# Issuing the output stores of a channel-attention and gated-convolution kernel from ScalarE's queue instead of SyncE's

## The chip, the core and the metric

The kernel runs on one core of one Trainium2 chip. The time is device microseconds for one execution of the program; the figure for a kernel is the median of its runs. In the profile, PE is TensorE, PEld its weight loads, DVE VectorE, ACT ScalarE, POOL GpSimd and SP SyncE; "SPq" and "ACTq" are instructions that SP and ACT carry out in their own queues, above all the issuing of transfers, and they aren't counted as busy time.

## The reference

Two stages, one behind the other, for 4 batches of 6336 rows and 256 channels, in float32:

```
qn = q / (norm(q, axis=1) + 1e-06);  kn = k / (norm(k, axis=1) + 1e-06)
s = kn.transpose(0, 2, 1) @ qn / tau            # 256 x 256 per batch
a = softmax of s over its last axis
x = v @ a                                       # 6336 x 256 per batch
gate = sigmoid(sum over 5 taps of conv_w[k] * x shifted by 4 - k rows)
out = (gate * (x @ w_val)) @ w_out
```

## The kernel before

The first stage takes q and k in groups of three blocks of 128 rows. For each group, ACT rounds the data to the format that TensorE multiplies fast (`hi`, L435), POOL computes the remainder (`lo`, L438), PE adds the products hi·hi, hi·lo and lo·hi to `s_ps` (L494), ACT squares the group (L462), and DVE or POOL adds the squares (L466). At the end of a batch a chain of small operations on ACT, DVE, POOL and PE turns `s_ps` into the softmax and into the two matrices that the second stage multiplies by: L544 and L546 on PE, a square root on ACT (L562), reciprocals on DVE, the exponential (L588) and the division (L600) on ACT, a transposition on PE (L613), and so on. Square root, exponential and sigmoid each need an own function table on ACT, so going from one to another costs an ACT_TABLE_LOAD.

The second stage runs in 52 steps of at most 508 rows, 13 for each batch. The steps of batch b run interleaved with the first stage of batch b+1. A step loads v in four transfers (L690), DVE transposes it (L695), ACT rounds it (`v_hi`, L699), POOL takes the remainder (`v_lo`, L702), PE makes `x_ps` and `val_ps` (L710), ACT starts the convolution (L733) and DVE (with some help from ACT and POOL, L741 and L744) adds the taps (L736), ACT takes the sigmoid (L747), DVE multiplies by `val_ps` (L754), ACT rounds (`g_hi`, L760), POOL takes the remainder (`g_lo`, L763), and PE makes the output in two halves (`o_ps`, L782). ACT copies each half from PSUM to the tile `o_sb` (L791), and when both halves are there, two transfers store the step: one of 112 partitions and one of 15 (L796). The step before the last is stored half by half. The last step, of 240 rows, has its own copies and stores (L801, L803), one half on ACT and one on DVE and SP.

No line of the program orders this by hand. Each piece is a task with an engine, an estimated cost, its dependencies and the tile buffers that it takes and uses. A planner (`Plan.run`) gives each task a due time, worked out backwards from the order in which PE should do its work, and then places tasks engine by engine: of those that can start, the one due first. The order found in this way is the order of the instructions in each engine's queue, and each queue runs strictly in order. A task that issues transfers has its cost as a tuple (bytes, transfers, slowness); the planner counts 0.45 us of the issuing engine for each transfer. The number of `o_sb` buffers is 2, of q/k buffers (`raw`) 7, of `v_raw` 4, of `hi`/`lo` and of `v_hi`/`v_lo` 3 each.

```
task(("Y", n, p), "ACT", 0.48, lambda p=p: out_copy(p), deps=[("F", n, p)] ...)
task(("R", n), "SP", (w * C * 4, 2, 1), lambda: store(0, nt), deps=[("Y", n, p) ...], uses=[o_i])
```

One thing about transfers is needed below. Each transfer signals its end on one of eight semaphores, which show as DMAHW0 to DMAHW7 in the listing of waits; they are dealt out in turn over all transfers of the program, whichever queue issues them. A transfer that gets a semaphore waits until the transfer that had it before, eight places earlier in the program, has landed; the waiting is done by the queue that issues it.

Of the kernel before, what the change touches and what calls it, by code (L numbers as in the profile page):

```python
# [27 lines left out]
class Plan:  # L28
# [6 lines left out]
    def task(self, key, engine, cost, emit, deps=(), uses=(), takes=(), lead=(), table=None):  # L35
        assert key not in self.tasks, key
        self.tasks[key] = dict(key=key, engine=engine, cost=cost, emit=emit, deps=list(deps), lead=dict(lead), table=table, uses=list(dict.fromkeys(list(uses) + list(takes))),
                               takes=list(takes), order=len(self.tasks))
# [182 lines left out]
def kernel(  # L221
# [13 lines left out]
    nc = tc.nc  # L235
    B, N, C = q.shape
# [34 lines left out]
    task = plan.task  # L271
# [396 lines left out]
    def even(rows):  # L668

        whole_ = rows // 16 * 16 if rows % 15 else rows  # L670
        return [x for x in ((0, whole_), (whole_, rows)) if x[0] < x[1]]

    def step_tasks(n):

        b, i = all_steps[n]
        t0, w = chunks[i]
# [3 lines left out]
        t = {}  # L680
# [84 lines left out]
        nt = -(-w // P)  # L765
        rows = w // nt
        pairs = [range(j, min(j + (1 if end else 2), nt)) for j in range(0, nt, 1 if end else 2)]
# [17 lines left out]
        dst = out[b, t0:t0 + w].rearrange("(j r) c -> r j c", j=nt)  # L785
# [7 lines left out]

        def store(a, z):
            for r0, r1 in even(rows):
                nc.sync.dma_start(out=dst[r0:r1, a:z, :], in_=t["o_sb"][r0:r1, a:z, :])  # L796

        def out_end(u):
            copy, dma = ((nc.scalar.copy, nc.scalar), (nc.vector.tensor_copy, nc.sync))[u]
# [5 lines left out]
        v_i, vs_i, gate_i, g_i, o_i = ("v_raw", n), ("v", n), ("gate", n), ("g", n), ("o_sb", n)  # L805
# [4 lines left out]
        for h in range(NH):  # L810
            x_i = (("s_ps", "acc_ps")[h] if late else "x", n, h)
            if edge:
                task(("E", n, h), "DVE", 0.08, lambda h=h: margin(h), deps=[("M", b, "divide")] + ([("X", n - 1, h)] if n else []), uses=[x_i], takes=[x_i])
            task(("X", n, h), "PE", 1.385 * part, lambda h=h: mix(h), deps=[("W", n), ("M", b, "low")] + ([("E", n, h)] if edge else []),
                 uses=[vs_i, x_i], takes=[] if edge else [x_i],
                 lead={("W", n): first_lo if new else last_lo, ("M", b, "low"): last_lo if new else 0} if h == 0 else {})
            task(("G", n, h), "ACT", 0.06 + 0.51 * part, lambda h=h: gate(h), deps=[("X", n, h), ("ready", "conv")] + [("G", n, x) for x in range(h)],
                 uses=[x_i, gate_i], takes=[gate_i] if h == 0 else [])
# [5 lines left out]
            for k_ in range(1, few):  # L824
                task(("D", n, h, k_), "DVE", 0.08 + 0.57 * part, lambda h=h, k_=k_: tap(h, k_),
                     deps=[("D+", n) if few < K else ("G", n, h) if k_ == 1 else ("D", n, h, k_ - 1)] + ([("D", n, h, k_ - 1)] if few < K and k_ > 1 else []),
                     uses=[x_i, gate_i])
# [6 lines left out]
        if n >= NS - 2:  # L834
            for h in range(NH):
# [3 lines left out]
                     deps=[("H", n, h)], uses=[gate_i, g_i])  # L839
# [5 lines left out]
        for p in range(len(pairs)):  # L845
# [3 lines left out]
                 uses=[g_i, o_ps_i], takes=[o_ps_i], lead={x: (0.47 * len(pairs[p]) if HEADS else 0.47) for x in low_done} if p == 0 else {})  # L849
# [3 lines left out]
                task(("Y", n, p), "ACT", 0.48, lambda p=p: out_copy(p), deps=[("F", n, p)] + [("Y", n, x) for x in range(p)], uses=[o_ps_i, o_i], takes=[o_i] if p == 0 else [])  # L853
        if n == NS - 2:
            for p, pair in enumerate(pairs):
                task(("R", n, p), "SP", (len(pair) * rows * C * 4, 2, 1), lambda pair=pair: store(pair[0], pair[-1] + 1), deps=[("Y", n, p)], uses=[o_i])
        elif not end:
            task(("R", n), "SP", (w * C * 4, 2, 1), lambda: store(0, nt), deps=[("Y", n, p) for p in range(len(pairs))], uses=[o_i])
        t["pairs"] = [("F", n, p) for p in range(len(pairs))]
        return t["pairs"]  # L860

# [6 lines left out]
    for b in range(B):  # L868
        softmax_tasks(b)
    outs = [step_tasks(n) for n in range(NS)]  # L870


# [85 lines left out]
```

## Time and profile before

| | |
|---|---|
| time, three runs | 591.70, 591.97 and 593.29 us, median 591.97 |
| the profiled execution | 593.26 us, its span from first to last instruction 591.5 us |
| DVE busy | 514.3 us, 87% |
| TensorE's granted clock | 1.000 over the span |
| transfers | 105.83 MB; the 16 DMA engines are at 8 to 9 tenths in the first quarter of the span and at 2 to 6 tenths in the last |
| the chain that ended last | 89% PE, 6% DMA, 1% each of ACT, POOL, issuing and SP's queue |

The chain of work that ended last goes through loads of q, k and v until 58.6 us; from there to the end of PE's work it is PE and nothing else.

### The profile page before, as it was taken

The page shows a single profiled execution, that of the slowest core. Times are in us where ns is not written, and L with a number is a line of the kernel's source. Part 1 is how long each engine was busy: PE and PEld are TensorE (multiplying, and loading weights), DVE is VectorE, ACT ScalarE, POOL GpSimd, SP SyncE. Part 2 cuts the span into 40 slices and gives each one's busy share as a digit, 9 for nine tenths or more (in the row PEclk, how much of TensorE's full clock was granted, in tenths as well). Part 3 has the DMA queues.
Part 4 walks back from the last instruction along what each step waited for, and adds up shares of the span by engine and source line. Part 5 has one row for each costly group of instructions (what it writes and reads, how often), then busy time and mean ns, then how long its engine had stood idle before and what let it go on. Part 6 is the DMA issues. An engine that isn't in the chain of part 4 may idle for free.

```text
span 591.5 us, 10511 instructions
## 1 busy us (share of the span) xinstructions
PE 585.7 (99%) x3667; PEld 531.2 (90%) x3667; DVE 514.3 (87%) x792; ACT 479.6 (81%) x582; POOL 506.3 (86%) x241
## 2 busy tenths in 40 slices
PE   9999999999999999999999999999999999999997
PEld 8898899998989999998989998998998998888887
DVE  3996899999989899988788899988969989988774
ACT  6698989889899979787798989788559777767754
POOL 4997999999997999999887999999935778777743
PEclk9999999999999999999999999999999999999999
DMA  8999997958577797874766899678333464553214
GB/s 331 383 368 231 273 243 200 213 133 226 169 157 179 203 214 195 169 190 112 219 166 153 208 213 244 143 190 181 75 93 103 114 160 118 124 141 89 68 40 123
DMA packets 154943, 105.83 MB, mean 179 GB/s; under 512 B 111114, under 2 KB 137994, under 8 KB 154890
## 3 DMA queue, kind: packets, MB, share of 16 engines
q1 hardware_dynamic: 154467, 104.51, 68.7%
q8 instruction: 29, 0.48, 0.4%
q10 hardware_dynamic: 423, 0.65, 0.3%
q14 instruction: 24, 0.20, 0.1%
HBM read 79.18 MB, written 25.95 MB: 178 GB/s over the span
## 4 chain that ended last, share of the span: by engine, by line
PE 89%; DMA 6%; ACT 1%; POOL 1%; issue 1%; SPq 1%; DVE 0%; POOLq 0%; ACTq 0%
PE o_ps L782 24%; PE x_ps L710 23%; PE val_ps L710 23%; PE s_ps L494 17%; DMA raw<-in_q_dram 4%; PE o_ps L626 1%; DMA raw<-in_k_dram 1%; DMA v_raw<-in_v_dram 1%; ACT sq L462 1%; SPq L412 1%; PE o_ps L613 0%; POOL v_lo L702 0%; ACT hi L435 0%; POOL acc L466 0%; PE o_ps L546 0%
## 5 line engine op out<-in xcount | busy, mean ns | idle before, releaser
L736 DVE SCALAR_TENSOR_TENSOR gate<-x_ps,wa,gate 128x508 f32<-128x508 f32 (+1 forms) x400 | 271.2, 717 | 33.9 <-ACT gate L733 31.2
L438 POOL TENSOR_TENSOR lo<-raw,hi 128x1536 fp32r<-128x1536 f32 (+2 forms) x65 | 185.4, 2857 | 7.8 <-ACT hi L435 6.0
L702 POOL TENSOR_TENSOR v_lo<-v_raw,v_hi 128x1024 fp32r<-128x1024 f32 (+1 forms) x52 | 124.1, 2387 | 14.6 <-ACT v_hi L699 12.1
L763 POOL TENSOR_TENSOR g_lo<-gate,g_hi 128x1016 fp32r<-128x1016 f32 (+2 forms) x52 | 120.7, 2322 | 16.9 <-ACT g_hi L760 16.6
L466 DVE TENSOR_TENSOR acc_ps<-acc_ps,sq 128x512 f32<-128x512 f32 (+1 forms) x146 | 101.2, 693 | 21.0 <-ACT sq L462 17.1
L710 PE MATMUL x_ps<-v_hi,w 128*128 128x512 f32 (+2 forms) x416 | 110.1, 384 | 0.0
L710 PE MATMUL val_ps<-v_hi,w 128*128 128x508 f32 (+1 forms) x416 | 107.8, 380 | 0.0
L462 ACT ACTIVATE sq<-raw 128x1536 f32<-128x1536 f32 (+2 forms) x68 | 95.8, 1413 | 3.0 <-POOL acc L466 1.7
L435 ACT CAST hi<-raw 128x1536 fp32r<-128x1536 f32 (+2 forms) x65 | 78.9, 1216 | 19.8 <-PE s_ps L494 11.1
L710 PEld LDWEIGHTS val_ps<-v_hi,w 128*128 128x128 f32 x416 | 76.1, 188 | 14.9
L710 PEld LDWEIGHTS x_ps<-v_hi,w 128*128 128x128 f32 x416 | 72.9, 188 | 12.8 <-POOL w L607 0.4
L733 ACT ACTIVATE gate<-x_ps,wa 128x508 f32<-128x508 f32 (+1 forms) x104 | 68.5, 664 | 14.0 <-PE x_ps L710 13.7
L782 PE MATMUL o_ps<-wo_hi,g_hi 128*127 128x256 f32 (+1 forms) x396 | 79.3, 282 | 0.0
L782 PE MATMUL o_ps<-wo_lo,g_hi 128*127 128x256 f32 (+1 forms) x396 | 79.0, 281 | 0.0
L494 PE MATMUL s_ps<-lo,hi 128*128 128x256 f32 x310 | 78.5, 287 | 0.0
L494 PE MATMUL s_ps<-hi,lo 128*128 128x256 f32 x310 | 77.2, 283 | 0.0
L791 ACT COPY o_sb<-o_ps 127x512 f32<-127x512 f32 (+1 forms) x99 | 57.8, 587 | 23.5 <-PE o_ps L782 23.1
L754 DVE TENSOR_TENSOR gate<-val_ps,gate 128x508 f32<-128x508 f32 (+1 forms) x104 | 67.4, 655 | 4.3 <-ACT gate L747 3.1
L699 ACT CAST v_hi<-v_raw 128x1024 fp32r<-128x1024 f32 (+1 forms) x52 | 57.5, 1107 | 16.0 <-PE val_ps L710 16.0
L466 POOL TENSOR_TENSOR acc<-acc,sq 128x512 f32<-128x512 f32 x46 | 59.9, 1301 | 10.9 <-ACT sq L462 9.6
L747 ACT ACTIVATE gate<-gate 128x1016 f32<-128x1016 f32 (+1 forms) x52 | 53.2, 1022 | 16.2 <-DVE gate L736 15.9
L782 PEld LDWEIGHTS o_ps<-wo_hi,g_hi 128*127 128x127 f32 (+1 forms) x396 | 62.7, 187 | 2.6
(96 smaller groups left out, 948.7 us busy)
## 6 DMA issues: line engine op xcount, KB each, us to landing
raw<-in_q_dram SPq DMA_DIRECT2D x64, 384.0 KB, 5.9
v_raw<-in_v_dram SPq DMA_DIRECT2D x192, 128.0 KB, 5.3
raw<-in_k_dram SPq DMA_DIRECT2D x63, 384.0 KB, 6.2
out_dram<-o_sb SPq DMA_DIRECT2D x47, 448.0 KB, 3.2
out_dram<-o_sb SPq DMA_DIRECT2D x47, 60.0 KB, 3.0
v_raw<-in_v_dram SPq DMA_DIRECT2D x16, 64.0 KB, 2.4
out_dram<-o_sb SPq DMA_DIRECT2D x3, 240.0 KB, 2.7
raw<-in_q_dram SPq DMA_DIRECT2D x4, 128.0 KB, 4.0
```

Source lines behind the costliest of these rows:

```text
L435: nc.scalar.copy(t["hi"][r, js], t["raw"][r, js, :, :])
L438: nc.gpsimd.tensor_tensor(t["lo"][r, js], t["raw"][r, js, :, :], t["hi"][r, js].bitcast(F32), ALU.subtract)
L462: nc.scalar.activation(t["sq"][0:np_, ja:jb], t["raw"][0:np_, ja:jb], AF.Square)
L466: eng.tensor_tensor(st[key][0:np_], st[key][0:np_], t["sq"][0:np_, j], ALU.add)
L494: nc.tensor.matmul(st["s"][:, h, :], lhs, rhs, start="open" not in st, stop=stop)
L702: nc.gpsimd.tensor_tensor(t["vl"][:, :, 0:g, :], t["v"], t["vh"][:, :, 0:g, :].bitcast(F32), ALU.subtract)
L710: nc.tensor.matmul(dst, weights[b][:, which, ws, ch, hs], vs[:, ch, at + lo:at + hi_], start=n_ == 0, stop=n_ == len(ops) - 1)
L733: nc.scalar.activation(t["gate"][:, h, 0:w], t["x", h][:, 0:w], AF.Copy, scale=cw[:, h, 0:1])
L736: nc.vector.scalar_tensor_tensor(t["gate"][:, h, 0:w], t["x", h][:, k_:k_ + w], cw[:, h, k_:k_ + 1], t["gate"][:, h, 0:w], ALU.mult, ALU.add)
L754: nc.vector.tensor_tensor(t["gate"][:, h, 0:w], t["val", h][:, 0:w], t["gate"][:, h, 0:w], ALU.mult)
L763: eng.tensor_tensor(t["gl"][:, hs, 0:w], t["gate"][:, hs, 0:w], t["gh"][:, hs, 0:w].bitcast(F32), ALU.subtract)
L782: nc.tensor.matmul(t["o", p][0:rows, u * C:(u + 1) * C], gs[:, h, j * rows:(j + 1) * rows], ws[:, h, :], start=(u, n_) == (0, 0) if HEADS ...
```

## The change

The two stores of each step are issued by ACT instead of SP, and the planner is told so: the task "R" runs on engine ACT. The stores of the last step (L803) stay as they were.

```
         def store(a, z):
             for r0, r1 in even(rows):
-                nc.sync.dma_start(out=dst[r0:r1, a:z, :], in_=t["o_sb"][r0:r1, a:z, :])
+                nc.scalar.dma_start(out=dst[r0:r1, a:z, :], in_=t["o_sb"][r0:r1, a:z, :])
...
         if n == NS - 2:
             for p, pair in enumerate(pairs):
-                task(("R", n, p), "SP", (len(pair) * rows * C * 4, 2, 1), lambda pair=pair: store(pair[0], pair[-1] + 1), deps=[("Y", n, p)], uses=[o_i])
+                task(("R", n, p), "ACT", (len(pair) * rows * C * 4, 2, 1), lambda pair=pair: store(pair[0], pair[-1] + 1), deps=[("Y", n, p)], uses=[o_i])
         elif not end:
-            task(("R", n), "SP", (w * C * 4, 2, 1), lambda: store(0, nt), deps=[("Y", n, p) for p in range(len(pairs))], uses=[o_i])
+            task(("R", n), "ACT", (w * C * 4, 2, 1), lambda: store(0, nt), deps=[("Y", n, p) for p in range(len(pairs))], uses=[o_i])
```

Because the planner works with the new engine, more than the stores moves. All 101 store transfers go from SP's queue to ACT's. Five of the additions of squares (L466) go from DVE to POOL (142 and 46 before; 137 and 51 after, of the 128-partition ones). ACT gets two more table loads, one for the sigmoid (L747) and one for the exponential (L588). PE does the same matrix products in a partly different order.

The first place is ACT's queue in the third step that stores, some 100 to 110 us into the span; o_sb is the output tile, hi the rounded q and k, and the waits that an instruction has are in brackets. Before, its rows were:

```order
L733 ACTIVATE gate<-x_ps,wa 128x508 [waits PE_49]
L462 ACTIVATE sq<-raw 128x1536 [waits DVE_49,Activation_49]
L699 CAST v_hi<-v_raw 128x1024 [waits DMAHW5_49,DMAHW4_49,DMAHW6_49,DMAHW3_49,PE_49]
L791 COPY o_sb<-o_ps 127x512 [waits DMAHW7_49,DMAHW0_49,PE_49]
L791 COPY o_sb<-o_ps 127x512 [waits PE_49]
L747 ACTIVATE gate<-gate 128x1016 [waits DVE_49]
L760 CAST g_hi<-gate 128x1016 [waits DVE_49,Activation_49]
```

With the change the same stretch of ACT's queue reads:

```order
L462 ACTIVATE sq<-raw 128x1536 [waits DVE_49]
L733 ACTIVATE gate<-x_ps,wa 128x508 [waits PE_49]
L462 ACTIVATE sq<-raw 128x1536 [waits DVE_49]
L699 CAST v_hi<-v_raw 128x1024 [waits DMAHW5_49,DMAHW4_49,DMAHW6_49,DMAHW3_49,PE_49]
L791 COPY o_sb<-o_ps 127x512 [waits PE_49] x2
L796 DMA out_dram<-o_sb 112x4x256 [waits DMAHW4_49,Activation_49]
L796 DMA out_dram<-o_sb 15x4x256 [waits DMAHW6_49]
L760 CAST g_hi<-gate 128x1016 [waits DVE_49]
L747 ACTIVATE gate<-gate 128x1016
L435 CAST hi<-raw 128x1536 [waits DMAHW3_49,PE_49,Pool_49]
```

Two issues now stand between the copies and the rounding of the next step's gate. The semaphore that the first of them waits for, DMAHW4, was last used by the load of k of the same stretch, the second row here, from SP's queue with the change:

```order
L412 DMA raw<-in_q_dram 128x768 [waits DMAHW3_49,Activation_49]
L412 DMA raw<-in_k_dram 128x768 [waits DMAHW4_49]
L690 DMA v_raw<-in_v_dram 32x16x64 [waits DMAHW5_49,Pool_49]
L690 DMA v_raw<-in_v_dram 32x16x64 [waits DMAHW6_49]
L690 DMA v_raw<-in_v_dram 32x16x64 [waits DMAHW7_49]
L690 DMA v_raw<-in_v_dram 32x16x64 [waits DMAHW0_49]
```

That pair of loads waits for the first of the two squarings shown in ACT's queue (L462), which frees the buffer that it fills. So the store's issue on ACT waits for a load that ACT itself released five of its instructions earlier.

The second place is ACT's queue in the softmax of the second batch, from the dummy exponential that brings the table (L578) to the division (L600). Before:

```order
L578 ACTIVATE dummy<-ones 128x1
L791 COPY o_sb<-o_ps 127x512 [waits PE_49]
L462 ACTIVATE sq<-raw 128x1536 [waits DMAHW1_49,DMAHW2_49,DVE_49,Pool_49]
L588 ACTIVATE s,o_ps<-s,m 128x256 [waits DVE_49]
L588 ACTIVATE s,o_ps<-s,m 128x256 [waits Activation_49]
L760 CAST g_hi<-gate 128x1016 [waits DVE_49]
L600 ACTIVATE a<-s,rz 128x256 [waits DVE_49]
```

With the change:

```order
L578 ACTIVATE dummy<-ones 128x1
L699 CAST v_hi<-v_raw 128x2x256 [waits DMAHW7_49,DMAHW1_49]
L435 CAST hi<-raw 128x1536 [waits DMAHW7_49,PE_49,Pool_49]
L733 ACTIVATE gate<-x_ps,wa 128x508 [waits PE_49,Pool_49]
L747 ACT_TABLE_LOAD
L747 ACTIVATE gate<-gate 128x1016 [waits DVE_49]
L588 ACT_TABLE_LOAD
L588 ACTIVATE s,o_ps<-s,m 128x256 [waits DVE_49]
L588 ACTIVATE s,o_ps<-s,m 128x256 [waits Activation_49]
L791 COPY o_sb<-o_ps 127x512 [waits PE_49]
L796 DMA out_dram<-o_sb 112x4x256 [waits DMAHW7_49,Activation_49]
L796 DMA out_dram<-o_sb 15x4x256 [waits DMAHW0_49]
```

A sigmoid has moved in ahead of the exponential, with the two table loads that this takes, and a store behind it. PE's order there moves too: between L546 and L613 it has 50 products of `s_ps` where it had 18.

The third place is the end of ACT's queue. Before, the last rows were:

```order
L791 COPY o_sb<-o_ps 127x512 [waits DMAHW1_49,DMAHW0_49,PE_49]
L747 ACTIVATE gate<-gate 128x2x240 [waits DVE_49]
L791 COPY o_sb<-o_ps 127x512 [waits PE_49]
L760 CAST g_hi<-gate 128x240 [waits DVE_49,Pool_49]
L791 COPY o_sb<-o_ps 127x512 [waits DMAHW3_49,DMAHW2_49,PE_49]
L760 CAST g_hi<-gate 128x240 [waits DVE_49]
L791 COPY o_sb<-o_ps 127x512 [waits PE_49]
L801 COPY o_end<-x_ps 120x256 [waits PE_49]
L803 DMA out_dram<-o_end 120x256 [waits Activation_49]
```

With the change, from the sigmoid of the last step on:

```order
L747 ACTIVATE gate<-gate 128x2x240 [waits DVE_49]
L796 DMA out_dram<-o_sb 112x4x256 [waits Activation_49]
L796 DMA out_dram<-o_sb 15x4x256
L760 CAST g_hi<-gate 128x240 [waits DVE_49,Pool_49]
L791 COPY o_sb<-o_ps 127x512 [waits DMAHW3_49,DMAHW2_49,PE_49]
L760 CAST g_hi<-gate 128x240 [waits DVE_49]
L791 COPY o_sb<-o_ps 127x512 [waits PE_49]
L796 DMA out_dram<-o_sb 112x2x256 [waits Activation_49]
L796 DMA out_dram<-o_sb 15x2x256
L796 DMA out_dram<-o_sb 112x2x256 [waits Activation_49]
L796 DMA out_dram<-o_sb 15x2x256
L801 COPY o_end<-x_ps 120x256 [waits PE_49]
```

The four issues for the step before the last now stand between its last copy and the last step's own copy and store. PE's last rows are the same in both.

## The prediction

> **What bounds the kernel now.** I read the page's busy times first, then the busy time of each engine in stretches of the span.
>
> ```profile
> span 591.5 us, 10511 instructions
> PE 585.7 (99%) x3667; PEld 531.2 (90%) x3667; DVE 514.3 (87%) x792; ACT 479.6 (81%) x582; POOL 506.3 (86%) x241
> ...
> 100.00:200.00 100.00, 100.00 (x649) 91.19 (x648) 96.16 (x150) 90.86 (x107) 96.55 (x43) 1.00 0.71 175
> 100.00:400.00 300.00, 300.00 (x1956) 274.38 (x1955) 275.47 (x419) 261.46 (x302) 287.55 (x121) 1.00 0.76 184
> 400.00:570.00 170.00, 170.00 (x1024) 151.65 (x1023) 146.24 (x215) 125.27 (x170) 125.26 (x61) 1.00 0.45 112
> 70.00:587.60 517.60, 517.60 (x3300) 470.02 (x3298) 462.58 (x697) 423.36 (x515) 449.06 (x196) 1.00 0.65 161
> ```
>
> The columns of a stretch are its length, then PE, PEld, DVE, ACT and POOL. From 70 us to its last product at 587.6 us, PE is busy for 517.60 of 517.60 us. It is the bound, and it has no idle time to give back there. From 100 to 200 us ACT and POOL are nearly full too (90.86 and 96.55 of 100), so a stage that feeds PE has little room there. From 400 us on both have a quarter of their time free.
>
> Next, the waits: who waited for whom, total, times, longest.
>
> ```profile
> ACT o_sb L791 <- PE o_ps L782: 23.1, 33, 2.9
> ...
> SPq L796 <- ACT o_sb L791: 259.8, 50, 9.9
> SPq L412 <- DMA raw<-in_q_dram: 8.5, 12, 2.1
> ```
>
> SP stood 259.8 us at stores, waiting for ACT's copies, with the loads queued behind. That looks like something to win, but PE lost nothing by it after 70 us, and the first store goes out only at 85 us (the first row of the next fence). So the change can gain nothing in the body, and the question is what it costs. The third row matters too: SP's loads wait 12 times for an earlier load of q to land. These are waits at issue, and on SP nobody sees them.
>
> **Term 1: the issues on ACT.** The store's line in the whole span, from 100 to 400 us and from 400 to 570 us, SP's loads of q after 84 us, and the two other lines that issue on ACT (minimum, median, maximum in ns, then first and last start):
>
> ```profile
> L796 SPq DMA_DIRECT2D out_dram<-o_sb x101: 317/352/1846, 85.4 to 587.2; - x101
> ...
> L796 SPq DMA_DIRECT2D out_dram<-o_sb x52: 328/424/1052, 108.5 to 398.1; - x52
> ...
> L796 SPq DMA_DIRECT2D out_dram<-o_sb x37: 317/348/504, 409.0 to 567.8; - x37
> ...
> L412 SPq DMA_DIRECT2D raw<-in_q_dram x41: 328/814/3482, 88.1 to 398.6; - x41
> ...
> L412 ACTq DMA_DIRECT2D raw<-in_k_dram x2: 418/438/457, 0.7 to 1.2; - x2
> ...
> L803 ACTq DMA_DIRECT2D out_dram<-o_end x1: 667/667/667, 587.4 to 587.4; - x1
> ```
>
> From 100 to 400 us an issue holds the queue for 0.42 us on SP; on ACT the trace has only three, 0.44 twice and 0.67 once. I take 0.44, the row nearest to a full stretch of issues, and keep 0.67 as the upper end; below 0.32 none was seen. There are 26 stores from 100 to 400 us, so 8 or 9 in 100 us: 16 issues x 0.44 = 7.0 us from 100 to 200.
>
> **Term 2: two more table loads,** both on ACT in the second batch's softmax, between 170 and 190 us.
>
> ```profile
> 182.50 0.67 ACT L733 ACTIVATE gate<-x_ps,wa 128x508 f32<-128x508 f32 x1
> 183.19 1.28 ACT L747 ACT_TABLE_LOAD   x1
> 184.49 1.05 ACT L747 ACTIVATE gate<-gate 128x1016 f32<-128x1016 f32 x1
> ```
>
> The load begins 0.02 us after the activation ahead of it ends and the next one follows 0.02 us behind, so each costs 1.28 us, and two 2.6 us. The Trainium skill, "ScalarE: Activation LUTs", section "What ACT_TABLE_LOAD costs", adds a drain of about 1380 ns to each switch; by that the two would be 5.3 us and the sum some 2.7 us higher. The trace shows no such gap here, so the row stands.
>
> **Term 3: waits for a semaphore's previous transfer.** A store's issue waits until the transfer eight places earlier has landed. On SP that was free; on ACT all of its work stands behind. In the first place shown, that earlier transfer is the load of k which ACT's squaring releases. The timeline of before at that place, and the issues' median time to landing (last number):
>
> ```profile
> 101.61 1.48 ACT L462 ACTIVATE sq<-raw 128x1536 f32<-128x1536 f32 x1
> ...
> 107.93 0.59 ACT L791 COPY o_sb<-o_ps 127x512 f32<-127x512 f32 x1 [0.83 <-PE o_ps L782]
> ...
> 103.12 0.36 SPq L412 DMA_DIRECT2D raw<-in_q_dram  x1
> 103.52 0.43 SPq L412 DMA_DIRECT2D raw<-in_k_dram  x1
> 104.05 1.97 SPq L690 DMA_DIRECT2D v_raw<-in_v_dram  x4
> ...
> v_raw<-in_v_dram SPq DMA_DIRECT2D x192, 128.0 KB, 5.3
> raw<-in_k_dram SPq DMA_DIRECT2D x63, 384.0 KB, 6.2
> ```
>
> The squaring ends at 103.09 and the load of q goes out at once; k goes out at 103.52 and lands at 103.52 + 6.2 = 109.7. The copy that the store needs ends at 108.52. So ACT stands for about 1.2 us, between 0 and 3 as landings vary. The second issue waits for the second of the four v loads, 104.05 + 0.5 + 5.3 = 109.9, by when the first has only just gone out: nothing more. By the changed order, four of the stores from 100 to 200 us have a load of the same step eight places earlier, released five or six ACT instructions ahead: 4 x 1.2 = 4.8 us (0 to 12). Others have an earlier store or a load long landed there and cost nothing.
>
> **What of it reaches PE.** From 100 to 200 us ACT needs 90.86 + 7.0 + 2.6 + 4.8 = 105.3 of 100 us, so it falls 5.3 us behind. Three buffers of `hi` and `v_hi` cover a delay of that size, but the tightest link does not: `g_lo`, made by POOL from ACT's `g_hi` just ahead of the product that uses it.
>
> ```profile
> 122.31 2.46 POOL L763 TENSOR_TENSOR g_lo<-gate,g_hi 128x1016 fp32r<-128x1016 f32 x1
> ...
> 128.26 2.86 PE o_ps L782 x24
> ```
>
> It ends at 124.8 and the product begins at 128.3: 3.5 us in hand. So PE loses 5.3 - 3.5 = **1.8 us**, between 0 (loads land a little earlier) and 5.3 (nothing in hand). Afterwards ACT catches up: from 200 to 400 us it had 170.6 us of work and gets 36 x 0.44 = 15.8 us more, 186.4 of 200.
>
> The second place, as a check within that: between norms and transposition ACT gains a rounding of v (0.65), a gate (0.67), a sigmoid (1.05), two loads (2.57) and a store (0.88), 5.8 us.
>
> ```profile
> 172.28 0.65 ACT L699 CAST v_hi<-v_raw 128x512 fp32r<-128x512 f32 x1
> ...
> 181.69 0.90 ACT L600 ACTIVATE a<-s,rz 128x256 f32<-128x256 f32 x2
> ...
> 183.60 0.60 PE L613 MATMUL o_ps<-ident,a 128*128 128x128 f32 x4
> ...
> 185.62 4.56 PE s_ps L494 x38
> ```
>
> The division would end at 182.6 + 5.8 = 188.4, or 0.9 earlier if its small waits close. PE has 32 more products ahead of the transposition, at 4.56/38 = 0.12 us: 183.6 + 3.8 = 187.4. It waits 0.1 to 1.0 us, part of the 1.8.
>
> ```profile
> L466 POOL TENSOR_TENSOR acc<-acc,sq 128x512 f32<-128x512 f32 x46 | 59.9, 1301 | 10.9 <-ACT sq L462 9.6 <-ACT acc L457 0.5
> ```
>
> POOL gets five additions more, 5 x 1.30 = 6.5 us; from 100 to 400 us it then has 294 of 300. I cost it at nothing, since DVE (275 of 300) loses the same five. If that cover is gone, it is the same lateness of `g_lo`, within the range above. After 400 us ACT has 125.3 of 170 us, and 37 issues add 16 us: nothing.
>
> **Term 4: the end.**
>
> ```profile
> 582.24 0.60 ACT L747 ACTIVATE gate<-gate 128x480 f32<-128x480 f32 x1 [1.00 <-DVE gate L736]
> ...
> 586.26 0.59 ACT L791 COPY o_sb<-o_ps 127x512 f32<-127x512 f32 x1 [0.58 <-PE o_ps L782]
> 586.97 0.37 ACT L801 COPY o_end<-x_ps 120x256 f32<-120x256 f32 x1
> 587.37 0.67 ACTq L803 DMA_DIRECT2D out_dram<-o_end  x1
> ...
> 588.13 0.35 SPq L803 DMA_DIRECT2D out_dram<-o_end  x1
> ...
> out_dram<-o_end ACTq DMA_DIRECT2D x1, 120.0 KB, 2.2
> out_dram<-o_end SPq DMA_DIRECT2D x1, 120.0 KB, 2.0
> ```
>
> Before, the last transfers land at 587.37 + 2.2 = 589.6 and 588.13 + 2.0 = 590.1. Now the sigmoid stands behind both copies and a store behind it, which makes the last roundings some 0.8 us and PE's last products 0.3 to 0.5 us later, so the last copy to `o_sb` ends at about 587.1. Four issues follow, 4 x 0.44 = 1.8, then the copy (0.37): the last store goes out at 589.3 and lands at 591.5. That is 591.5 - 590.1 = **1.4 us**, 1 to 2.3 (at 0.67 per issue).
>
> **The sum.** 1.8 + 1.4 = 3.2 us. The profiled execution took 593.26 us, 1.8 us more than its span, so it would take 596.5; the median of the three runs is 591.97, 1.3 us lower than that execution, and on it I forecast **595.2 us**. From 0.0 + 1.0 to 5.3 + 2.3 the forecast's own range is 593.0 to 599.6.
>
> **The rivals.**
> - *The body hides it all.* The planner has counted 0.45 us for each issue, about what the rows show, and PE went through 517 us without a stall, so the buffers take more than I count. For it: the terms that the planner doesn't know are only the 4.8 us of landings, and 3.5 us are in hand at the tightest link. Against it: ACT at 105 of 100. Then only the end is paid: 591.97 + 1.4 = 593.4, not slower as far as can be measured (within 0.3%, which is 590.2 to 593.7, and about what a measurement of this kernel can tell from no change). It decides from landings under 5 us or more than 5.3 us in hand.
> - *Issues on ACT are slow because SP issues at the same time.* For it: the one store on ACT took 0.67 us where SP's on the same line took 0.35, and SP's loads of q take up to 3.48 us to issue after 100 us. Against it: the two loads on ACT at 0.7 us ran beside SP's and took 0.44. At 0.67 per issue ACT needs 90.86 + 10.7 + 2.6 + 4.8 = 109.0 of 100 us, so PE loses 5.5, the end costs 2.3, and a few long issues of 2 to 3 us on ACT's path would add: about 8 us, 600 us. "Perfetto Trace Analysis" of the Trainium skill, section "DMA Instruction — HWDGE", speaks for this one: the descriptor generator is locked for one issuer at a time, and the shown time of an issue includes waiting for that lock. The single issue of 0.67 us agrees with it, the two of 0.44 us beside SP's own don't show it.
> - *Loads freed on SP.* With no store to stand behind, loads go out earlier and PE runs quicker. For it: 259.8 us of waits on SP. Against it: PE has no idle time from 70 to 587.6 us for it to fill, and the store's path at the end is only longer. It would take the whole cost of the end being hidden and the products themselves running closer: 590 us at best.
>
> **How the numbers follow.** Forecast 0.47, hidden 0.34, slow issues 0.15, freed loads 0.04. Slower by over 0.3% is above 593.7: nearly all of the forecast and the slow issues, 0.60; within 0.3%: the hidden case and the lowest of the forecast, 0.36; faster: 0.04. The range takes in the hidden case, the forecast and most of the slow issues: 592.3 to 601.5 us.
>
> **What would show it.** Right: ACT's queue with 101 issues of L796 at about 0.44 us; ACT waiting for transfers (raw or v_raw) at L796, around 1 us each, a few times from 100 to 200 us; PE idle for 1 to 3 us there, ahead of L782 or L613; last store out about 1.3 us later after PE's end. Wrong: PE busy without a gap to its end (then the body hides it), or issues of 0.6 us and more, with PE's idle time spread to 400 us. SP's waits at L796 vanish in any case.

## The result, and the profile after

| | before | changed |
|---|---|---|
| median, runs of the first comparison | 592.00 us (10 runs, 591.62 to 593.29) | 595.28 us (10 runs, 593.75 to 598.97) |
| ratio, 95% interval | | 1.0061 (1.0046 to 1.0076) |
| median in two later comparisons of the same two kernels | 591.91 and 592.07 us (17 runs each) | 594.25 us (5 runs) and 594.95 us (4 runs) |
| their ratios | | 1.0044 (1.0032 to 1.0056), 1.0046 (1.0032 to 1.0059) |
| profiled execution, its span | 593.26, 591.5 us | 595.32, 593.3 us |

The change costs 0.3 to 0.8% by the three intervals, 2.3 to 3.3 us by the medians: slower by more than a measurement of this kernel leaves open, and the forecast was 595.2. Three executions at a lower granted clock (638.62 us of the changed kernel, 637.34 and 968.19 us of the kernel before) are left out of all medians here. The profile after, first the page's busy times:

```profile
span 593.3 us, 10450 instructions
...
PE 586.7 (99%) x3667; PEld 531.2 (90%) x3667; DVE 511.6 (86%) x787; ACT 480.0 (81%) x584; POOL 512.3 (86%) x246
```

By stretches of the span (length, then PE, PEld, DVE, ACT, POOL):

```profile
100.00:200.00 100.00, 99.19 (x641) 90.05 (x640) 91.45 (x140) 87.43 (x105) 96.84 (x44) 1.00 0.73 197
100.00:400.00 300.00, 299.19 (x1949) 273.10 (x1948) 275.03 (x416) 262.47 (x303) 291.81 (x125) 1.00 0.69 189
400.00:570.00 170.00, 169.75 (x1022) 150.96 (x1021) 143.89 (x212) 123.63 (x168) 126.44 (x63) 1.00 0.40 102
70.00:589.00 519.00, 517.94 (x3298) 469.24 (x3296) 459.54 (x691) 422.72 (x516) 454.48 (x200) 1.00 0.60 160
```

PE, full without a gap before, now has 1.06 us of idle time in the body (519.00 - 517.94), 0.81 of it from 100 to 200 us. Who was waited for, from 84 to 580 us:

```profile
ACT g_hi L760 <- DMA v_raw<-in_v_dram: 2.5, 1, 2.5
...
ACT g_hi L760 <- DMA out_dram<-o_sb: 1.2, 1, 1.2
...
PE o_ps L782 <- POOL g_lo L763: 0.8, 1, 0.8
...
PE x_ps L710 <- DVE gate L736: 0.2, 1, 0.2
```

PE waits once for `g_lo` (0.8 us, at 189 us) and once for the convolution (0.2 us, at 455 us). ACT, which never waited for a transfer in this stretch before, does so behind two stores by this list: 2.5 us behind the one at 120 us, 1.2 us behind another. The list puts each idle stretch of an engine down to one event, and the time of the issues is in it. How long ACT's queue really stood for a transfer can be worked out from the times at which the trace shows transfers landing: seven issues begin within 0.1 us of the landing of the transfer whose semaphore they get, after standing for 4.9 us in all, 1.5 of it at the first store (85 us) and 3.4 from 100 to 200 us. The store's line, in the whole span and from 100 to 400 us:

```profile
L796 ACTq DMA_DIRECT2D out_dram<-o_sb x101: 323/362/2827, 85.2 to 589.0; - x101
...
L796 ACTq DMA_DIRECT2D out_dram<-o_sb x53: 323/341/544, 99.5 to 399.0; - x53
```

An issue on ACT takes 0.34 us in the full stretch, less than the 0.42 on SP before. SP's waits at L796, 259.8 us, are gone; SP waits for `v_lo` instead (216.5 us), and nobody gains by it. The end, on ACT's and SP's queues:

```profile
587.72 0.59 ACT L791 COPY o_sb<-o_ps 127x512 f32<-127x512 f32 x1 [0.58 <-PE o_ps L782]
587.73 1.81 ACTq L796 DMA_DIRECT2D out_dram<-o_sb  x4
589.59 0.37 ACT L801 COPY o_end<-x_ps 120x256 f32<-120x256 f32 x1 [1.27 <-PE x_ps L782]
589.99 0.35 ACTq L803 DMA_DIRECT2D out_dram<-o_end  x1
```

The four issues take 1.81 us and stand ahead of the last copy, as forecast. But the first pair runs while the last copy to `o_sb` runs, so that 1.23 us are left behind its end. And before, the last store out was SP's, 0.88 us behind the start of the row with PE's last products (588.13 and 587.25 us); now it is ACT's, 1.27 us behind it (589.99 and 588.72). Of the time of the issues 0.39 us is in the way.

### The profile page after: what moved, and what is told of

Same layout as the page of the kernel before. It is cut to its first block, busy times and chain, and to the rows that moved or that the text cites. A ratio compares the mean times of both kernels' runs of the same rounds, so it can differ in the third digit from the quotient of the medians.

```text
span 593.3 us, 10450 instructions
## 1 busy us (share of the span) xinstructions
PE 586.7 (99%) x3667; PEld 531.2 (90%) x3667; DVE 511.6 (86%) x787; ACT 480.0 (81%) x584; POOL 512.3 (86%) x246
## 4 chain that ended last, share of the span: by engine, by line
PE 81%; DMA 6%; POOL 4%; ACT 3%; DVE 3%; issue 2%; ACTq 1%; SPq 0%; DVEq 0%; POOLq 0%
PE o_ps L782 22%; PE x_ps L710 22%; PE val_ps L710 21%; PE s_ps L494 15%; DMA raw<-in_k_dram 6%; DVE gate L736 2%; POOL acc L466 1%; POOL lo L438 1%; ACTq L796 1%; PE o_ps L626 1%; ACT hi L435 1%; SPq L412 0%; POOL g_lo L763 0%; ACT o_sb L791 0%; ACT gate L747 0%
## 5 line engine op out<-in xcount | busy, mean ns | idle before, releaser
L710 PE MATMUL x_ps<-v_hi,w 128*128 128x512 f32 (+2 forms) x416 | 110.4, 385 | 0.3 <-DVE gate L736 0.2
L466 DVE TENSOR_TENSOR acc_ps<-acc_ps,sq 128x512 f32<-128x512 f32 (+1 forms) x141 | 97.6, 692 | 13.4 <-ACT sq L462 9.3
L710 PE MATMUL val_ps<-v_hi,w 128*128 128x508 f32 (+1 forms) x416 | 107.8, 380 | 0.0
L462 ACT ACTIVATE sq<-raw 128x1536 f32<-128x1536 f32 (+2 forms) x68 | 95.6, 1411 | 3.8 <-POOL acc L466 2.3
L710 PEld LDWEIGHTS val_ps<-v_hi,w 128*128 128x128 f32 x416 | 75.8, 188 | 14.6
L710 PEld LDWEIGHTS x_ps<-v_hi,w 128*128 128x128 f32 x416 | 72.5, 188 | 13.8 <-issue 0.6
L733 ACT ACTIVATE gate<-x_ps,wa 128x508 f32<-128x508 f32 (+1 forms) x104 | 67.8, 660 | 16.2 <-PE x_ps L710 6.8
L782 PE MATMUL o_ps<-wo_hi,g_hi 128*127 128x256 f32 (+1 forms) x396 | 79.2, 281 | 0.0
L782 PE MATMUL o_ps<-wo_lo,g_hi 128*127 128x256 f32 (+1 forms) x396 | 79.0, 281 | 0.0
L466 POOL TENSOR_TENSOR acc<-acc,sq 128x512 f32<-128x512 f32 x51 | 67.1, 1315 | 10.0 <-ACT sq L462 8.8
L760 ACT CAST g_hi<-gate 128x1016 fp32r<-128x1016 f32 (+3 forms) x54 | 53.0, 983 | 19.4 <-DVE gate L754 10.3
L782 PEld LDWEIGHTS o_ps<-wo_hi,g_hi 128*127 128x127 f32 (+1 forms) x396 | 62.8, 187 | 2.8
```

Of the source, the lines that this page charges most:

```text
L462: nc.scalar.activation(t["sq"][0:np_, ja:jb], t["raw"][0:np_, ja:jb], AF.Square)
L466: eng.tensor_tensor(st[key][0:np_], st[key][0:np_], t["sq"][0:np_, j], ALU.add)
L710: nc.tensor.matmul(dst, weights[b][:, which, ws, ch, hs], vs[:, ch, at + lo:at + hi_], start=n_ == 0, stop=n_ == len(ops) - 1)
L733: nc.scalar.activation(t["gate"][:, h, 0:w], t["x", h][:, 0:w], AF.Copy, scale=cw[:, h, 0:1])
L782: nc.tensor.matmul(t["o", p][0:rows, u * C:(u + 1) * C], gs[:, h, j * rows:(j + 1) * rows], ws[:, h, :], start=(u, n_) == (0, 0) if HEADS ...
```

## The experiments

The changed kernel does three things at once: a new order on all engines, issues on ACT in the body, and issues on ACT at the end. The first four experiments take them apart.

**e1: the new order alone.** The planner still places the stores on ACT, but SP issues them.

```
-                nc.scalar.dma_start(out=dst[r0:r1, a:z, :], in_=t["o_sb"][r0:r1, a:z, :])
+                nc.sync.dma_start(out=dst[r0:r1, a:z, :], in_=t["o_sb"][r0:r1, a:z, :])
```

> The order of the changed kernel on PE, DVE, POOL and ACT, but the 101 stores are issued by SP again. Theory P (the planner's new order costs the time: three additions of squares on POOL just ahead of g_lo, two more table loads): PE still waits about 0.8 us for g_lo near 189 us, and the median stays at 594.3 to 595.0; only the issues at the end, some 0.6 us, are won back. Theory I (ACT's time for the issues costs it): without 101 x 0.36 us on ACT the waits of PE vanish and the median is 592.0 to 592.5, that of the kernel before.

Measured: 592.74 us (592.24 to 593.19, 11 runs) beside 592.02 for the kernel before, ratio 1.0011 (1.0002 to 1.0019). PE's wait for `g_lo` is gone; what stays is the one for the convolution, 0.3 us. So the new order costs 0.7 us, of which the waits show 0.3, and the wait at 189 us isn't the order's alone. Theory P falls for the larger part; the range of theory I is missed too, by 0.2 us.

**e2: the issues alone,** with the order of before:

```
-                nc.sync.dma_start(out=dst[r0:r1, a:z, :], in_=t["o_sb"][r0:r1, a:z, :])
+                nc.scalar.dma_start(out=dst[r0:r1, a:z, :], in_=t["o_sb"][r0:r1, a:z, :])
```

> The order of the kernel before on every engine, with the 101 stores issued by ACT, which the planner doesn't know of. Theory P: PE is busy without a gap to its end in the body, and only the end is paid: 592.3 to 593.0. Theory I: ACT falls behind where it has no room, more than in the changed kernel since nothing was planned for it: PE idle for over 1 us from 100 to 400 us, and 595 to 598.

Measured: 601.49 us (600.33 to 602.20, 4 runs), ratio 1.0154 (1.0141 to 1.0168), three times the cost of the whole change, and above the ranges of both theories. The waits of PE and the end of ACT's timeline in e2:

```profile
PE x_ps L710 <- DVE gate L736: 1.8, 2, 1.0
PE o_ps L782 <- POOL g_lo L763: 1.6, 2, 1.2
PE x_ps L782 <- ACT g_hi L760: 0.8, 1, 0.8
PE o_ps L782 <- ACT g_hi L760: 0.8, 1, 0.8
```

```profile
589.62 0.87 ACTq L796 DMA_DIRECT2D out_dram<-o_sb  x2
590.58 0.39 ACT L760 CAST g_hi<-gate 128x240 fp32r<-128x240 f32 x1 [1.00 <-ACT o_sb L791]
```

PE waits 5.0 us in six places, the last ones for roundings (L760) that stand behind a store's issues in ACT's queue. In the order of before the copies stand ahead of these roundings, and with the stores on SP no issue came behind a copy. The changed kernel, whose order was planned for the issues, is 6.2 us quicker than e2: that the planner was told is worth more than the whole remaining cost.

**e3: the end on SP.** As the changed kernel, with the last six transfers issued by SP.

```
-                nc.scalar.dma_start(out=dst[r0:r1, a:z, :], in_=t["o_sb"][r0:r1, a:z, :])
+                (nc.sync if n >= NS - 3 else nc.scalar).dma_start(out=dst[r0:r1, a:z, :], in_=t["o_sb"][r0:r1, a:z, :])
```

> As the changed kernel, but the last six of the 101 store transfers (the two steps before the last) are issued by SP; the order of PE, DVE, POOL and of ACT's other work is the same. If the end costs the 1.4 us of the prediction: 593.9. If it costs the 0.6 us that the trace shows behind PE's end: 594.7. If the issues between the last roundings also delay PE's last products, PE's end comes 0.3 to 0.5 us earlier as well.

Measured: 594.02 us (592.52 to 597.43, 12 runs), ratio 1.0038 (1.0022 to 1.0053). Run once more, 594.09 (593.01 to 596.25, 9 runs) beside 594.95 for the changed kernel:

> e3 on the same chip as the changed kernel. The end by the traces is 0.6 us (last store landed, counted from the start of PE's last product: 3.5 us against 2.9): 0.6 us below the changed kernel, 593.6 to 594.7, still with runs above 595. If the end is worth 1.3 us, as the medians of two different chips gave it, 1.3 below.

The end is worth 0.9 us by these medians (1.3 against the first comparison). By the traces it is 0.7: from the start of the row with PE's last two products to the end of the execution (its time less that start) the five profiles with the end on SP (e1, e3 twice, e5, e9) take 5.83 to 6.04 us, mean 5.95, the four with it on ACT and otherwise unchanged or with other semaphores (the changed kernel three times, e8) 6.45 to 6.89, mean 6.65. Both are more than the 0.6 that I expected from the first trace, and less than the 1.4 of the prediction.

**e4: POOL's additions behind `g_lo`.** In the changed kernel three additions (L466) stand just ahead of the late `g_lo`. They are moved behind it, and nothing else is.

```
+        late = [x for x in order if x[1][:3] == ("A", 2, 2) and x[2] == "POOL"]; order = [y for x in order if x not in late for y in ([x] + late if x[1] == ("J", 9) else [x])]
```

> As the changed kernel, but on POOL three additions of squares stand behind one g_lo near 186 us instead of ahead of it; nothing else moves. Theory P: g_lo ends about 3.9 us earlier, PE's wait of 0.8 us for it near 189 us vanishes with nothing in its place, and the median falls by about 0.8 us, to 594.5. Theory I: ACT is what is late, so g_lo waits for g_hi instead, or the wait comes back at the next product; the median stays at 595.3.

Measured: 596.23 us (594.49 to 596.72, 5 runs), ratio 1.0060 (1.0047 to 1.0073): nothing won. Its POOL and PE timelines, and the rounding on ACT in the changed kernel and in e4:

```profile
187.18 2.40 POOL L763 TENSOR_TENSOR g_lo<-gate,g_hi 128x1016 fp32r<-128x1016 f32 x1 [2.99 <-ACT g_hi L760]
...
230.30 0.74 PE L782 MATMUL o_ps<-wo_hi,g_lo 128*127 128x256 f32 x4 [1.06 <-POOL g_lo L763]
```

```profile
185.26 1.05 ACT L760 CAST g_hi<-gate 128x1016 fp32r<-128x1016 f32 x1 [0.95 <-DVE gate L736]
...
186.06 1.04 ACT L760 CAST g_hi<-gate 128x1016 fp32r<-128x1016 f32 x1 [0.95 <-DVE gate L736]
```

POOL stands idle for 2.99 us, has the additions to do behind `g_lo`, and PE's wait turns up 41 us later instead. `g_lo` begins at 187.18, against 187.19 with the additions ahead, but that is a coincidence of two executions: in the changed kernel `g_hi` was there at 186.31, 0.88 us before POOL began `g_lo` behind the additions, and in e4's profile, which was later than that from the first store on (its issues begin at 85.99 us instead of 85.17), at 187.10. So the additions do stand in the way at 189 us; moving them only moves the wait, because POOL has no time for them behind `g_lo` either (it has no gap from 187 to 235 us).

These four leave 1.3 us (e3 against e1) for issuing on ACT in the body. Either ACT's time is what costs (theory T) or its standing behind transfers (theory W).

**e5: ACT's time without transfers.** SP issues the stores; at the same places ACT makes a copy for each transfer.

```
+                n < NS - 3 and nc.scalar.copy(burn[0:120], zeros[0:120].bitcast(F32)); nc.sync.dma_start(out=dst[r0:r1, a:z, :], in_=t["o_sb"][r0:r1, a:z, :])
```

> The order of the changed kernel, the stores issued by SP, and in the place of each store's issue on ACT a copy of 120x256 to a tile that nobody reads (about 0.37 us; not in the last two storing steps before the end). [...] To be compared with e1 (592.74) and e3 (594.02). Theory T (ACT's time is what costs): 594.0 to 595.5, with PE waiting in the body for 1 to 3 us. Theory W (what costs is that ACT's queue now stands behind transfers: long issues of 1.4 to 2.8 us, which come at other places in each execution): 592.7 to 593.2, runs within 1 us of each other as in e1.

Measured: 592.63 us (592.03 to 593.54, 11 runs), ratio 1.0012 (1.0003 to 1.0020), the time of e1. A stretch of e5, and the copies:

```profile
100.00:200.00 100.00, 100.00 (x655) 91.53 (x654) 90.39 (x139) 93.80 (x122) 97.42 (x44) 1.00 0.74 178
```

```profile
L796 ACT COPY burn<-zeros x95: 388/407/440, 84.2 to 576.4; 120x256 f32<-120x256 f32 x95
```

95 copies of 0.41 us, a pair of them 0.85 us where a pair of issues mostly takes 0.87, and PE is busy for 100.00 of 100 us with ACT at 93.80. **This amount of ACT's time costs nothing.** Theory T falls, and with it the way in which the prediction reckoned. A queue that is held for 2 us in one place is not tested by this: the two copies ahead of the first late rounding take 0.85 us too.

**e6: one transfer per store** of 127 partitions instead of 112 and 15.

```
-            for r0, r1 in even(rows):
+            for r0, r1 in [(0, rows)]:
```

> As the changed kernel, but each store is one transfer of 127 partitions, so ACT issues 51 instead of 101. Half of the issue time in the body (1.3 us of the 3.3) and at the end (1.3) goes, if a single issue takes no longer: 594.0 by theory T. By theory W the second issue of a pair is the one that waits least, so the body keeps its 1.3 and only the end's half is won: 594.6; the runs still scatter by 4 us or more.

Measured: 1302.09 us (1301.42 to 1304.03, 6 runs). Neither theory had this; it tells nothing of them, and is taken up in the last section.

**e7: four transfers per store,** each of two of the step's four column blocks, except in the last two storing steps.

```
+            for r0, r1, a, z in [(*r, x, y) for r in even(rows) for x, y in (((a, (a + z) // 2), ((a + z) // 2, z)) if n < NS - 3 else ((a, z),))]:
```

> As the changed kernel, but each store but the last two steps' is issued in four transfers instead of two, so ACT issues 96 more in the body. Theory T: 96 x 0.35 = 34 us more on ACT, 5 to 6 us more of them from 100 to 200 us where it has no room; the body's 1.3 us become 4 to 7 us and the median 598 to 601. Theory W: only the number of places at which ACT can stand behind a transfer doubles: 596.5 to 597, and the runs scatter by 5 us or more.

Measured: 612.64 us (608.09 to 615.90, 6 runs), ratio 1.0343 (1.0313 to 1.0373), far above both expectations. Its waits:

```profile
ACT gate L733 <- DMA out_dram<-o_sb: 14.9, 9, 2.2
ACT g_hi L760 <- DMA out_dram<-o_sb: 14.4, 6, 4.9
...
ACT hi L435 <- DMA out_dram<-o_sb: 4.0, 6, 0.9
```

These three rows make 33.3 us in 21 places. The list names the stores themselves, but by the landings ACT's queue stood for earlier loads: 22 issues begin within 0.1 us of the landing of a load whose semaphore they get (16 of v, 3 of k, 3 of q), after 20.1 us in all; the rest is mostly the issues' own time. So the waits that theory W names exist. What they cost is not taken apart here: PE waits 10.1 us, its products take 8.3 us longer than in the changed kernel (595.0 us against 586.7, the granted clock at 0.7 and 0.8 of full speed in two of the page's 40 slices), and 96 more issues take ACT's time as well.

The changed kernel was run twice again:

> The changed kernel once more, on the same chip as the three others: 595.3, between 593.7 and 599. If its body's loss comes from fixed places, PE waits for g_lo near 189 us as in the first profile; if it comes from what each execution's transfers do, the wait is at another place or of another length.

> The changed kernel on the same chip as e8, e9 and e3: 594.2 to 595.3, PE's wait for g_lo near 189 us between 0.5 and 1 us.

594.25 us (5 runs) and 594.95 us (4 runs), both in the range of the first comparison. PE's wait for `g_lo` is at 189 us both times, 0.6 and 0.8 us long: its place is fixed, its length is not.

**e8: other semaphores.** In the program, loads that stood up to 9 us ahead of a store now come behind it; that deals the eight semaphores out anew. A dependency that only sets the program's order (no wait) holds it so, and every engine's queue has the same rows in the same order.

```
+    for r in [x for x in order if x[1][0] == "R"]:
...
+                n += T[order[j][1]]["cost"][1]
+                if n > limit or any(x[1] in after[order[j][1]] for x in order[j:i]):
+                    break
+                moved.insert(0, order[j])
...
+        order[i:i] = moved
...
+            plan.tc.add_manual_dep(i, last.name, mybir.DependencyInfo(mybir.DependencyClass.NoSync, mybir.DependencyReason.DATA), reason="turn")
```

> As the changed kernel, instruction by instruction on every engine, but the eight semaphores are dealt out in another order: the loads that the planner places up to 9 us ahead of a store, six transfers at most, come behind the store in the count, so that the transfer eight places ahead of a store is an older load or the store of the step before. Theory W (ACT stands in its stores' issues until a transfer eight places earlier has landed): ACT's waits of 2.5 us for a load of v at 121 us and of 1.2 us for a store vanish, so does PE's wait of 0.6 to 0.8 us for g_lo near 189 us, the median falls by about 1 us to 594.0 or less, and the runs lie within 1.5 us instead of 5. If issues on ACT are slow for another reason (the issuing itself, SP issuing at the same time), nothing changes: 594.3 to 595.3 with the same scatter.

Measured: 594.97 us (594.50 to 595.26, 5 runs), ratio 1.0046 (1.0034 to 1.0059), beside 594.95 for the changed kernel. Its waits:

```profile
PE o_ps L782 <- POOL g_lo L763: 0.8, 1, 0.8
PE x_ps L710 <- DVE gate L736: 0.3, 1, 0.3
```

ACT's waits of 2.5 and 1.2 us behind stores are gone, as they should be; by the landings no issue of a store stands for an earlier transfer any more. PE's wait for `g_lo` is as long as before, and so is the time. **Taking away the waits for the transfer eight places earlier wins nothing,** and theory W, as it was put, falls. At the first store that doesn't clear the waits, as the next part shows: there a long issue takes the wait's place. (e8 also has a price of its own: the next loads of q and k get the first store's semaphores and go out at 90.43 us, where the changed kernel issues that load of q at 83.73.)

**e9: both,** e8 with the end on SP, `(nc.sync if n >= NS - 3 else nc.scalar)` as in e3.

> As e8, with the last six store transfers on SP as in e3. If order (0.7 us over the kernel before, by e1), waits in the stores' issues and the end are all that there is, this is e1 again, with nearly all stores on ACT: 592.5 to 593.0, within 1 us. Above 593.5, issuing on ACT costs something in the body that is neither these waits nor ACT's time.

Measured: 593.94 us (592.78 to 594.26, 9 runs), ratio 1.0024 (1.0015 to 1.0034): 1.0 below e8, the end once more, and 1.2 above e1. Something in the body was left that is neither the sum of ACT's time nor these waits alone.

**What the traces show in its place.** The changed kernel's timeline at the first store, ACT and POOL, then POOL and PE at 189 us:

```profile
85.17 2.18 ACTq L796 DMA_DIRECT2D out_dram<-o_sb  x2
87.39 1.05 ACT L760 CAST g_hi<-gate 128x1016 fp32r<-128x1016 f32 x1 [2.54 <-DVE v_raw L695]
...
88.52 2.40 POOL L763 TENSOR_TENSOR g_lo<-gate,g_hi 128x1016 fp32r<-128x1016 f32 x1 [0.96 <-ACT g_hi L760]
...
187.19 4.78 POOL L763 TENSOR_TENSOR g_lo<-gate,g_hi 128x1016 fp32r<-128x1016 f32 x2
...
189.62 0.74 PE L782 MATMUL o_ps<-wo_hi,g_lo 128*127 128x256 f32 x4 [0.79 <-POOL g_lo L763]
```

The same places in e1, SP first:

```profile
84.12 3.66 SPq L796 DMA_DIRECT2D out_dram<-o_sb  x2
...
86.74 2.44 POOL L763 TENSOR_TENSOR g_lo<-gate,g_hi 128x1016 fp32r<-128x1016 f32 x1
...
185.18 4.82 POOL L763 TENSOR_TENSOR g_lo<-gate,g_hi 128x1016 fp32r<-128x1016 f32 x2
...
187.66 0.74 PE L782 MATMUL o_ps<-wo_hi,g_lo 128*127 128x256 f32 x4
```

The two issues of the first store hold any queue for long: 2.18 us on ACT here, 3.66 on SP in e1, 2.62 on SP before. What happens in that time isn't the same everywhere. The two issues of the changed kernel one by one, with the load of k that has the second one's semaphore before it (its issue and, in the row behind that, its size and its time to landing), then the two of e8:

```profile
81.06 0.43 SPq L412 DMA_DIRECT2D raw<-in_k_dram  x1
...
raw<-in_k_dram SPq DMA_DIRECT2D x1, 384.0 KB, 5.7
...
85.17 0.37 ACTq L796 DMA_DIRECT2D out_dram<-o_sb  x1
...
86.76 0.59 ACTq L796 DMA_DIRECT2D out_dram<-o_sb  x1
```

```profile
84.64 0.37 ACTq L796 DMA_DIRECT2D out_dram<-o_sb  x1
...
85.06 1.83 ACTq L796 DMA_DIRECT2D out_dram<-o_sb  x1
```

The issues of the changed kernel take 0.37 and 0.59 us; between them ACT's queue stands for 1.22 us until the load lands, 81.06 + 5.7 = 86.76. That is the wait of theory W. In e8 nothing is waited for, and the second issue itself takes 1.83 us. So neither alone is what makes the first store long.

On ACT the first store holds up `g_hi`, and POOL stands idle for 0.96 us ahead of `g_lo`. From there POOL has no time to make that up. Its busy time from 88 to 188 us, in the kernel before, in e1 and in the changed kernel (POOL's is the fifth busy time of the row, the one after ACT's):

```profile
88.00:188.00 100.00, 100.00 (x640) 90.83 (x639) 96.00 (x143) 89.52 (x104) 97.07 (x43) 1.00 0.76 186
```

```profile
88.00:188.00 100.00, 100.00 (x644) 91.09 (x643) 92.73 (x139) 88.36 (x103) 99.61 (x44) 1.00 0.76 187
```

```profile
88.00:188.00 100.00, 99.97 (x640) 90.64 (x640) 92.52 (x139) 88.84 (x104) 98.86 (x43) 1.00 0.78 211
```

97.07 of 100 us before, 99.61 with the new order. In e1 the first of the two `g_lo` ends at 185.18 + 2.41 (half of 4.82) = 187.59 and PE's product begins at 187.66: nothing is in hand there. DVE is held up by the first store as well, by way of ACT's L733, and through it POOL idles once more, 0.20 to 0.25 us ahead of the `g_lo` near 110 us. The changed kernel there, ACT and POOL:

```profile
110.09 1.05 ACT L760 CAST g_hi<-gate 128x1016 fp32r<-128x1016 f32 x1 [2.13 <-DVE gate L754]
...
111.28 2.40 POOL L763 TENSOR_TENSOR g_lo<-gate,g_hi 128x1016 fp32r<-128x1016 f32 x1 [0.23 <-ACT g_hi L760]
```

So whatever POOL loses at 88 and 110 us reaches PE at 189 us undiminished. Nine profiles with this order on POOL and two transfers to a store show it by degrees. PE's products are the same in the same order in all nine, so the last column can set each beside e1, product by product: how much further behind e1 PE is at 198 us than it was at 82 us, ahead of the first store. Lengths in us.

| kernel | queue, from the start of the first store's two issues to their end | of it, standing for a load | POOL idle near 88 us | and near 110 us | PE's wait for `g_lo` near 189 us | PE further behind e1, from 82 to 198 us |
|---|---|---|---|---|---|---|
| e1 | SP, 3.66 | 0 | 0 | 0 | 0 | 0 |
| e5 | SP, 2.01 | 0 | 0 | 0 | 0 | -0.14 |
| e3 | ACT, 1.30 | 0.35 | 0 | 0.21 | 0 | 0.16 |
| e3 again | ACT, 1.80 | 0.84 | 0.44 | 0.20 | 0.5 | 0.59 |
| changed, second profile | ACT, 2.05 | 0.24 | 0.63 | 0.25 | 0.6 | 0.84 |
| e9 | ACT, 2.13 | 0 | 0.80 | 0.21 | 0.8 | 0.95 |
| changed, first profile | ACT, 2.18 | 1.22 | 0.96 | 0.23 | 0.8 | 1.20 |
| changed, third profile | ACT, 2.21 | 0.70 | 0.71 | 0.22 | 0.8 | 1.03 |
| e8 | ACT, 2.24 | 0 | 0.90 | 0.23 | 0.8 | 1.06 |

POOL's two idle stretches together are the last column to within 0.15 us in every row, and with the issues on SP neither occurs. That is the chain as far as traces can show it. It was not tried by itself: a kernel with the first store alone on SP, or alone on ACT, would settle it and hasn't run.

The rest of what separates e9 from e1 can be read off in the same way. In their two profiles e9's PE ends 1.30 us behind e1's: 0.22 of that stands there at 82 us already, before any store (the three profiles of the changed kernel stand 0.19 to 0.76 us behind e1 there); 0.95 is the chain; 0.13 comes at 322 us, ahead of an L710, as it does in the other six of the nine profiles that have the stores on ACT in the body, and in neither e1 nor e5. For e3 against e1 the traces explain less: e3's profiled execution took 593.12 us, 0.9 us less than the median of its runs, and what the slower ones lose was not seen.

No version beats the kernel before. e1 and e5, with all stores on SP, come nearest, 0.7 us above it.

## Why the prediction was right

The total was right to 0.1 us in the first comparison (595.28) and to 1.0 us in the two later ones (594.25 and 594.95), and the split in body and end was right in kind. That the sum came out so closely is partly luck: the body's 1.9 us hold 0.7 us of an order that the prediction priced at nothing, and the end was forecast too high.

- **The bound: right.** PE had nothing to win, and SP's 259.8 us of waits were worth nothing. The rival of freed loads falls with e1 against the changed kernel.
- **Term 1, the issues: right in kind, 0.34 us for 0.44, but not what costs.** From 100 to 200 us 16 issues take 6.3 us, 7.0 forecast. e5 puts about as much time on ACT and PE doesn't notice.
- **Term 2, two table loads: 1.28 us each, right.** Both stand in e1's order as well, where PE doesn't wait; the drain of the Trainium skill ("ScalarE: Activation LUTs", section "What ACT_TABLE_LOAD costs") doesn't show behind them after the change either (a sigmoid begins 0.01 us after its load ends, at 180.26 us).
- **Term 3, the waits: right in kind and nearly in size, but not where they cost.** From 100 to 200 us the first profile has 3.4 us of them by the landings (4.8 forecast), for loads of k and v behind three stores; the distance of POOL and DVE to e1 doesn't grow there, so they cost nothing. The first store, at 85 us, which the term leaves out, has 1.5 us more, for loads of q and k, and there they are part of what costs: 0.24 to 1.22 us of its length in the three profiles of the changed kernel. They aren't the only cause, since in e8 and e9 the store is as long without them.
- **What of it reaches PE: 1.8 us forecast, about 1.9 measured** (0.7 by the new order in e1, 1.2 to 1.3 by issuing on ACT in e3 and e9), at the link and in the place that were named, `g_lo` ahead of L782. The step that failed is "ACT needs 105.3 of 100 us, so it falls 5.3 us behind", less "3.5 us in hand". ACT's total isn't what makes `g_lo` late, and the 3.5 us were read at 122 us from the order of before, while the new order has 0.1 us in hand at 189 us. As far as the traces show it, the lateness came from one store at 85 us, ahead of the stretch that I summed, and the 5.3 - 3.5 that gave 1.8 met the measured time by luck. Of the signs that I named, the waits at L796 came (five from 100 to 200 us), PE's idle time there is 0.81 us where I had 1 to 3, and the last store goes out 0.39 us later behind PE's end, not 1.3.
- **"I cost it at nothing": the additions on POOL.** The cover that I named (DVE loses the same five) doesn't help POOL, which is the engine without room. POOL at 99.61 of 100 us is what carries the lateness for 100 us. This is the step that I should have priced.
- **Term 4, the end: 1.4 us forecast, 0.7 by the traces and 0.9 to 1.0 by the medians.** I set all four issues behind the last copy; the first pair belongs to the other half and runs beside it, so that 1.23 us of the issues stand behind the copy where I had 1.8. The later last products that I added did not come: from 325 us to its end PE keeps the same distance to e1.
- **The rivals.** "The body hides it all" is wrong by the 1.9 us. "Issues slow because SP issues at the same time" fails: of the 101 issues in the first profile of the changed kernel 37 overlap an issue of SP and take 0.37 us in the median, 64 don't and take 0.34. Three take over 0.7 us, 1.73 us beside SP, 2.83 and 1.27 us not beside it, and e8's issue of 1.83 us at the first store has none of SP's beside it either.

## What to carry to other kernels

When work moves to another queue under a planner, measure the new order and the move apart: here the order alone cost 0.7 us, the move without it 9.5, and both together 2.3 to 3.3. What an engine's added time costs is decided by the fullest engine behind it, not by its own sum: look for the one with no idle time left, and for the one event ahead of it that it can't make up. Slack is a property of an order; read in the old one, it is no evidence for the new. And take a merged row apart before you call its instructions slow: 1.22 of the 2.18 us of "two issues" were a wait between them.

## What had not been expected of the hardware

**A store of 127 partitions in one transfer (e6) takes some 14 us to issue** (median), and the kernel takes 1302 us instead of 592; TensorE's granted clock is 0.752 in its profile, so PE's own 705 us are part of that. The first lines of its page, the store's line and two of its issues:

```profile
span 1302.1 us, 10429 instructions
...
PE 704.8 (54%) x3667; PEld 616.9 (47%) x3667; DVE 513.2 (39%) x787; ACT 475.7 (37%) x584; POOL 509.5 (39%) x246
```

```profile
L796 ACTq DMA_DIRECT2D out_dram<-o_sb x52: 230/13977/19486, 86.1 to 1273.8; - x52
...
502.74 13.23 ACTq L796 DMA_DIRECT2D out_dram<-o_sb  x1
...
525.31 14.24 ACTq L796 DMA_DIRECT2D out_dram<-o_sb  x1
```

The Trainium skill has a rule that fits, on the page "DMA: Bandwidth & Descriptors", section "Why a DMA increments its semaphore by 16 and not by 1": a transfer is spread over the largest number of engines up to 16 that divides its outermost size, and for 127 partitions that is one. The trace agrees: the semaphore of e6's store at 308.28 us is updated twice, at 327.73 and 354.49 us, that of a store of 112 partitions in the changed kernel (133.40 us) 16 times. That the issuing queue stands for so long is what this run shows. 112 and 15 partitions, as the kernel splits them, take 0.34 us each.

**The first store holds any queue for long,** 1.30 to 3.66 us for its two issues in the nine profiles above, where later pairs mostly take 0.87. In five of the seven profiles on ACT 0.24 to 1.22 us of that is a wait for an earlier load to land. In the four where nothing is waited for, one of the two issues is itself long: 3.07 us in e1, 1.63 in e5, 1.83 in e8, 1.73 in e9. The DMA engines are full there (a share of 1.01 from 70 to 100 us in the changed kernel's row); whether that is the cause was not tried.
